# Score matmuls on 64 rows instead of twice 32: q and k transposed as bf16, one head's 64 dims on 64 partitions

## The chip, the cores and the metric

One core of a Trainium2 chip. The metric is device time in microseconds (us), the median of several executions; the profile is one execution, and its span is about 2 us shorter than the time of the same execution. Clock means the share of full speed that TensorE's throttle granted. Engines: PE is TensorE, PEld its loading of weights, DVE VectorE, ACT ScalarE, POOL GpSimd, SP SyncE; a q behind a name (SPq) means the engine's instruction sequencer.

Fast and slow are states of a run: one that is over 1.5% above the fastest run of the same kernel counts as slow and is left out of ratios.

## The reference

```python
# 8 batches, 8 heads, 576 tokens, 64 dims, float32
q_d, k_d, v_d = (x.reshape(B, H, 144, 4, D).mean(axis=3) for x in (q, k, v))   # pooled over 4 tokens
out_d     = softmax(scale * q_d @ k_d.T) @ v_d            # 144 x 144, then repeated 4 times
out_local = softmax(where(|i - j| < 4, scale * q @ k.T, -1e9)) @ v
x = (repeat(out_d, 4) + out_local)                        # -> [4608 tokens, 512]
h = x @ w_in                                              # 512 -> 2048
out = (h * sigmoid(1.702 * h)) @ w_out                    # 2048 -> 512
```

## The kernel before

Tokens are worked on in nine groups of 512. Group g runs the two large products for its tokens (the prediction calls them MoE products) and, between their matmuls, the attention of batch g+1. "The group of batch 2" is group 1, and so on; groups 7 and 8 have no attention. VectorE transposes q and k, GpSimd pools them and v, TensorE computes scores, ScalarE takes exponentials.

A head of q is 576 x 64 numbers: 32 rows of 1152, 18 tokens each. A load by GpSimd brings 4 heads as bf16 onto 128 partitions. In this kernel VectorE transposes 32x32 blocks (one operation of 128x576 fp32 takes 1.24 to 1.25 us); taken as fp32, one element is a pair of bf16 dims. So a head lands on 32 partitions with dims 2p and 2p+1 side by side (the last index, `a`), and each score needs two matmuls of 32 rows that accumulate.

```python
def load_1(name, src, store, b, qd):                # 128 rows, 4 loads a batch (k, q; qd = 0, 1)
    t = ldp.tile([128, 1152], BF16, name=f"{name}b{qd}", tag=f"{name}b{qd}", bufs=2)
    nc.gpsimd.dma_start(out=t, in_=bass.AP(tensor=src.tensor,
        offset=src[b, 4 * qd].offset, ap=[[1152, 128], [1, 1152]]))
    store[b, qd] = t

def prep_1(name, b, qd):                            # 4 fp32 transpositions a batch
    ...
    nc.vector.transpose(out=t32.rearrange("p (i c) -> p c i", c=18),
        in_=store[b, qd].bitcast(FP32).rearrange("p (c d) -> p c d", c=18))

def scores(b, qd, barred=False):                    # 80 matmuls; scores_d (pooled) has 24
    for i in range(5):
        for a in range(2):
            for par in range(2):
                for r in range(4):                  # 4 heads
                    rows = slice(32 * r, 32 * r + 32)
                    nc.tensor.matmul(sp[r // 2][64 * par : 64 * par + 64, r % 2, 60 * i : 60 * i + 60],
                        lhsT=kT[b, qd][rows, k0 : k0 + 64, a], rhs=qT[b, qd][rows, q0 : q0 + 60, a],
                        start=(a == 0 ...), stop=(a == 1 ...), tile_position=(32 * r, 64 * par))
# the order of GpSimd's, VectorE's and SyncE's work in the group of batch b:
    if b > 2: load_v4(b)                            # v in rows of 4 tokens, for pooling (SyncE)
    prep_qk(b, 0); pool_qk(b, 0)
    load_qk(b + 1, 0); load_qk(b + 1, 1)
    prep_v(b); load_v(b + 1)
    prep_qk(b, 1); pool_qk(b, 1)
    prep_v4(b)                                      # pooled v: six operations of GpSimd
```

The softmax here doesn't subtract the row's maximum and nothing guards it: scores larger than these inputs give would overflow.

## Time and profile before

The kernel takes 330.7 us (median of 3 runs, 329.6 to 332.09); the profiled span is 329.5 us at a mean clock of 0.995.

| Quantity | Value | View |
|---|---|---|
| PE busy | 308.0 us, 93% | busy table of the page |
| share of PE in the chain that ended last | 87% | chain of the page |
| groups 1 to 6, start to start | 35.1, 33.7, 33.5, 33.4, 34.3, 33.4 us | starts of each group's first large matmul in the trace |
| a transposition (fp32, 128x576) | 1.24 to 1.25 us | groups of instructions |
| DMA share in a steady group | 0.68 | windows |

The lines of the page, before. First the busy table (time, share of the span, instructions), then the span in 40 slices, a digit being the busy share in tenths, then the chain that ended last:

```profile
PE 308.0 (93%) x4987; PEld 157.9 (48%) x5043; DVE 130.2 (40%) x215; ACT 184.1 (56%) x322; POOL 138.9 (42%) x168
...
PE   8767999789999999999999999998999999999995
...
DVE  4870512770468036802771277225730560000000
...
POOL 7890844049603970298029901990098000000000
PEclk9997999999999999999999999999999999999999
DMA  7999979999814991398339922993180110011011
...
PE 87%; issue 4%; SPq 3%; ACT 2%; DVE 2%; DMA 1%; DVEq 0%; ACTq 0%
```

From the tenth slice on PE is nearly full. VectorE, GpSimd and DMA each have pauses in every group. The costliest groups of instructions that the change touches, before (source line, engine, operation, out<-in, shapes, count | busy us, mean ns | idle before them and its cause):

```profile
L260 DVE STREAM_TRANSPOSE kT<-kb 128x576 f32<-128x576 f32 x16 | 20.0, 1249 | 2.0 <-DMA kb<-in_k_dram 2.0
L260 DVE STREAM_TRANSPOSE qT<-qb 128x576 f32<-128x576 f32 x16 | 19.8, 1239 | 0.9 <-DMA qb<-in_q_dram 0.7
```

The timeline of PE around one block of scores, before (start, length, and the count of matmuls merged into one line), and the windows view of one steady group (stretch, length, busy time of PE, PEld, DVE, ACT and POOL with instructions, clock, DMA share, GB/s; the DMA share adds up the time of packets over 16 engines, and can exceed 1):

```profile
146.25 1.03 PE L618 MATMUL pm<-xT,w_in_bf 128*128 128x512 bf16 x4
147.21 0.84 PE L351 MATMUL pa<-qT,kT 32*64 32x60 bf16 x80
147.85 0.59 PE L370 MATMUL pa<-qdT,kdT 32*64 32x144 bf16 x24
148.38 0.82 PE L618 MATMUL pm<-xT,w_in_bf 128*128 128x512 bf16 x2
```

```profile
135.90:169.40 33.50, 32.60 (x594) 16.88 (x600) 16.30 (x25) 20.95 (x36) 17.53 (x19) 1.00 0.68 144
```

The block of scores occupies PE from 147.21 to 148.38 us. VectorE is busy 16.3 of 33.5 us, GpSimd 17.5.

### The profile page before, as it was taken

To read this page: it belongs to the slowest core of one execution; us is meant where nothing else is said; L and a number is where in the kernel's file an instruction comes from. 1 tells how busy PE (TensorE), PEld (TensorE's weight loads), DVE (VectorE), ACT (ScalarE), POOL (GpSimd) and SP (SyncE) were. 2 spreads that over 40 slices of the span, in tenths; PEclk is the share of its full clock that TensorE was granted. 3 is DMA by queue.
4 is the path that set the end of the run, shared out by engine and by line. 5 is a ranking of instruction groups with operands and counts; after the bars stand their busy time and mean duration, and the time that the engine had idled before them with its cause. 6 is when DMAs were issued, how large, how long until landed. Compare 5 with 4: busy or idle time off the path is not lost.

```text
span 329.5 us, 11220 instructions
## 1 busy us (share of the span) xinstructions
PE 308.0 (93%) x4987; PEld 157.9 (48%) x5043; DVE 130.2 (40%) x215; ACT 184.1 (56%) x322; POOL 138.9 (42%) x168
## 2 busy tenths in 40 slices
PE   8767999789999999999999999998999999999995
PEld 3444455445554455455544555455444544444444
DVE  4870512770468036802771277225730560000000
ACT  2552773375936683667367746674566646415611
POOL 7890844049603970298029901990098000000000
PEclk9997999999999999999999999999999999999999
DMA  7999979999814991398339922993180110011011
GB/s 126 184 188 208 171 151 183 196 210 236 191 39 132 205 207 39 116 193 171 102 100 200 200 83 86 196 195 105 40 172 2 60 41 32 2 72 56 2 62 65
DMA packets 63552, 41.36 MB, mean 126 GB/s; under 512 B 44048, under 2 KB 54416, under 8 KB 63504
## 3 DMA queue, kind: packets, MB, share of 16 engines
q1 hardware_dynamic: 55056, 26.95, 35.8%
q0 software_dynamic: 8304, 13.63, 23.9%
q8 instruction: 39, 0.64, 0.9%
q14 instruction: 9, 0.07, 0.1%
q10 hardware_dynamic: 144, 0.07, 0.1%
HBM read 44.83 MB, written 9.44 MB: 165 GB/s over the span
## 4 chain that ended last, share of the span: by engine, by line
PE 87%; issue 4%; SPq 3%; ACT 2%; DVE 2%; DMA 1%; DVEq 0%; ACTq 0%
PE pm L618 35%; PE pm L674 33%; PE pa L351 3%; SPq L214 3%; PE pa L618 2%; PE pa L431 2%; PE pa L409 2%; PE pa L370 2%; PE pa L458 2%; PE pa L674 2%; DMA vf<-in_v_dram 1%; PE pm L689 1%; PE pa L484 1%; ACT vd L321 0%; PE pa L312 0%
## 5 line engine op out<-in xcount | busy, mean ns | idle before, releaser
L618 PE MATMUL pm<-xT,w_in_bf 128*128 128x512 bf16 x528 | 120.3, 380 | 1.4 <-DVE xT L561 0.7
L674 PE MATMUL pm<-w_out_bf,gT 128*128 128x512 bf16 x493 | 114.1, 379 | 5.4 <-issue 5.2
L629 ACT ACTIVATE gT<-pm 128x512 bf16<-128x512 f32 x136 | 81.0, 598 | 45.2 <-PE pm L618 45.2
L618 PEld LDWEIGHTS <-w_in_bf 128*128 128x128 bf16 x576 | 55.8, 98 | 68.4 <-issue 2.5
L674 PEld LDWEIGHTS <-gT 128*128 128x128 bf16 x560 | 51.7, 98 | 59.5 <-issue 0.2
L276 POOL TENSOR_TENSOR pq<-kT 128x576 f32<-128x576 bf16 x16 | 18.5, 1157 | 105.0 <-DVE kT L260 96.1
L395 DVE TENSOR_TENSOR es<-es,mask 128x600 bf16<-128x600 bf16 x28 | 20.6, 749 | 92.0 <-ACT es L381 91.2
L659 ACT ACTIVATE osb<-pm 128x512 f32<-128x512 f32 (+2 forms) x35 | 20.7, 592 | 40.2 <-PE pm L674 36.1
L534 ACT COPY od<-pa 128x384 f32<-128x384 f32 (+1 forms) x56 | 18.4, 412 | 32.4 <-DVE y L444 18.7
L444 DVE TENSOR_TENSOR y<-pa,rc 128x896 bf16<-128x896 f32 x32 | 34.9, 1092 | 1.1
L555 DVE TENSOR_TENSOR xT<-pa,od 128x570 bf16<-128x570 f32 x28 | 21.1, 753 | 12.0 <-ACT od L534 11.9
L381 ACT ACTIVATE es<-pa 128x600 bf16<-128x600 f32 x32 | 19.8, 668 | 7.0 <-PE pa L351 6.8
L297 POOL TENSOR_TENSOR v<-v 112x512 f32<-112x512 f32 x18 | 22.8, 1265 | 0.0
L661 DVE TENSOR_SCALAR osb<-pm 128x128 f32<-128x128 f32 x1 | 0.3, 292 | 55.3 <-ACT osb L659 55.3
L260 DVE STREAM_TRANSPOSE kT<-kb 128x576 f32<-128x576 f32 x16 | 20.0, 1249 | 2.0 <-DMA kb<-in_k_dram 2.0
L260 DVE STREAM_TRANSPOSE qT<-qb 128x576 f32<-128x576 f32 x16 | 19.8, 1239 | 0.9 <-DMA qb<-in_q_dram 0.7
L276 POOL TENSOR_TENSOR pq<-qT 128x576 f32<-128x576 bf16 x16 | 18.4, 1148 | 0.0
L291 POOL CAST vb<-vf 128x2560 bf16<-128x2560 f32 (+1 forms) x11 | 17.6, 1618 | 0.0
L442 DVE RECIPROCAL rc<-pa 128x14 f32<-128x14 f32 x32 | 7.7, 240 | 21.7 <-PE pa L431 21.7
L351 PE MATMUL pa<-qT,kT 32*64 32x60 bf16 x1280 | 14.0, 203 | 1.5 <-issue 1.5
L351 PEld LDWEIGHTS <-kT 32*64 32x64 bf16 x1280 | 11.8, 104 | 6.7 <-issue 5.5
L300 POOL TENSOR_TENSOR vd<-v 112x256 bf16<-112x256 f32 x18 | 13.7, 759 | 1.4
(90 smaller groups left out, 247.0 us busy)
## 6 DMA issues: line engine op xcount, KB each, us to landing
vf<-in_v_dram SPq DMA_DIRECT2D x80, 128.0 KB, 4.7
out_dram<-osb SPq DMA_DIRECT2D x35, 256.0 KB, 2.1
v<-in_v_dram SPq DMA_DIRECT2D x36, 192.0 KB, 6.1
kb<-in_k_dram POOLq DMA_DIRECT2D x16, 288.0 KB, 6.8
qb<-in_q_dram POOLq DMA_DIRECT2D x16, 288.0 KB, 7.1
w_out_bf<-in_moe_w_out_dram POOLq DMA_DIRECT2D x4, 512.0 KB, 12.1
w_in_bf<-in_moe_w_in_dram POOLq DMA_DIRECT2D x2, 512.0 KB, 5.7
w_in_bf<-in_moe_w_in_dram POOLq DMA_DIRECT2D x1, 1024.0 KB, 10.7
```

The costliest lines, as they stand in the source:

```text
L260: nc.vector.transpose(out=t32.rearrange("p (i c) -> p c i", c=18), in_=store[b, qd].bitcast(FP32).rearrange("p (c d) -> p c d", c=18),)
L276: nc.gpsimd.tensor_tensor(out=t1, in0=sv[:, :, 0:2, :], in1=sv[:, :, 2:4, :], op=ALU.add)
L297: eng.tensor_tensor(out=t1[0:112], in0=x[:, :, 0:2, :], in1=x[:, :, 2:4, :], op=ALU.add)
L351: nc.tensor.matmul(sp[r // 2][64 * par : 64 * par + 64, r % 2, 60 * i : 60 * i + 60], lhsT=kT[b, qd][rows, k0 : k0 + 64, a], rhs=qT[b, qd] ...
L381: nc.scalar.activation(out=es[2 * qd + u][:, :, 0:300], in_=sp[u][:, :, 0:300], func=AF.Exp, scale=inv_sqrt_d,)
L395: nc.vector.tensor_tensor(out=ev, in0=ev, in1=mask, op=ALU.mult)
L444: nc.vector.tensor_tensor(out=y, in0=ov[:, :, :, 0:D], in1=rc.to_broadcast([128, 2, 7, D]), op=ALU.mult,)
L555: eng.tensor_tensor(out=sub(xT[hp], t0 + 3, (57, 2), (114, 5), (1, 57)), in0=sub(x, 3, (509, 2), (57, 5), (1, 57)), in1=sub(od, 3, (57, 2) ...
L618: nc.tensor.matmul(acc, lhsT=w_in_bf[:, dmc, ffc * 128 : (ffc + 1) * 128], rhs=xT[dmc][:, g * TG : g * TG + TG], start=(dmc == 0), stop=(d ...
L629: nc.scalar.activation(out=gT[:, ffc, :], in_=acc, func=AF.Silu, scale=GELU_SCALE)
L659: eng.activation(out=osb, in_=ap, func=AF.Copy, scale=1.0 / GELU_SCALE)
L674: nc.tensor.matmul(ops[t], lhsT=gT[:, ffc, t * 128 : (t + 1) * 128], rhs=w_out_bf[:, ffc, :], start=(ffc == 0), stop=(ffc == n_ffc - 1),)
```

## The change

Its intent: with one head's 64 dims on 64 partitions a score is one matmul of 64 rows, so half of the score matmuls go. To get there, from batch 2 on each row is loaded twice into a pair of 32-partition blocks, the second copy half a token's dims (32 elements) further on, and VectorE transposes bf16 elements, 32 dims of each token. That makes 16 loads a batch (64 rows each) instead of 4, and 8 transpositions instead of 4. v is loaded head by head, and pooled a batch ahead.

```diff
+    ROWS64 = 2
+    def load_2(name, src, store, b, qd):
+        store[b, qd] = []
+        for u in range(2):
+            t = ldp.tile([128, 1152], BF16, ..., bufs=2)
+            store[b, qd].append(t)
+            for j in range(2):
+                nc.gpsimd.dma_start(
+                    out=t[64 * j : 64 * j + 64, 0:1120],
+                    in_=bass.AP(tensor=src.tensor, offset=src[b, 4 * qd + 2 * u + j].offset,
+                        ap=[[32, 2], [1152, 32], [1, 1120]]))
     def prep_1(name, b, qd):
+        if b >= ROWS64:
+            tt = tt.rearrange("p t a -> p (t a)").rearrange("p (u t) -> p u t", u=2)
+            for u in range(2):
+                nc.vector.transpose(
+                    out=tt[:, u].rearrange("p (i c) -> p c i", c=18),
+                    in_=store[b, qd][u].rearrange("p (c d) -> p c d", c=18)[:, :, 0:32])
     def scores(b, qd, barred=False):
+        if b >= ROWS64:
+            for u in range(2):
+                for i in range(5):
+                    for par in range(2):
+                        for j in range(2):
+                            rows = slice(64 * j, 64 * j + 64)
+                            nc.tensor.matmul(sp[u][64 * par : 64 * par + 64, j, 60 * i : 60 * i + 60],
+                                lhsT=kT[b, qd][rows, u, k0 : k0 + 64],
+                                rhs=qT[b, qd][rows, u, q0 : q0 + 60],
+                                start=True, stop=True, tile_position=(64 * j, 64 * par))
     ... scores_d, pool_qk and the uses of pooled v alike ...
@@ the order of the work
             loads_2()
+            prep_v4(2, nc.gpsimd)
         elif b < B:
-            if b > 2:
-                load_v4(b)
+            if b + 1 < B:
+                load_v4(b + 1)
             prep_qk(b, 0)
             pool_qk(b, 0)
             if b + 1 < B:
-                for qd in range(NQ):
-                    load_qk(b + 1, qd)
+                load_qk(b + 1, 0)
+            prep_qk(b, 1)
+            pool_qk(b, 1)
             prep_v(b, nc.gpsimd)
             if b + 1 < B:
                 load_v(b + 1)
-            prep_qk(b, 1)
-            pool_qk(b, 1)
-            prep_v4(b, nc.gpsimd)
+                load_qk(b + 1, 1)
+                prep_v4(b + 1, nc.gpsimd)
```

More of the change, by code (lines that the diff above doesn't have):

```diff
@@ L66 @@
     kdT = [persist.tile([128, 160, 2], BF16, name=f"kdT{i}") for i in range(NQ)]
+    kdP = [persist.tile([128, 2, 160], BF16, name=f"kdP{i}") for i in range(NQ)]
     PA = [psum.tile([128, 2, 512], FP32, name=f"pa{i}") for i in range(3)]
@@ L124, in fill @@
             nc.vector.memset(t[:, SD:160, :], 0.0)
+        for t in kdP:
+            nc.vector.memset(t[:, :, SD:160], 0.0)
         for t in vbs:
@@ L201, in load_1 @@
         store[b, qd] = t
+    def load_2(name, src, store, b, qd):
+        store[b, qd] = []
+        for u in range(2):
+            t = ldp.tile(
+                [128, 1152], BF16, name=f"{name}b{qd}", tag=f"{name}b{qd}", bufs=2
+            )
+            store[b, qd].append(t)
+            for j in range(2):
+                nc.gpsimd.dma_start(
+                    out=t[64 * j : 64 * j + 64, 0:1120],
+                    in_=bass.AP(
+                        tensor=src.tensor, offset=src[b, 4 * qd + 2 * u + j].offset,
+                        ap=[[32, 2], [1152, 32], [1, 1120]],
+                    ),
+                )
     def load_qk(b, qd):
-        load_1("k", k, kf, b, qd)
-        load_1("q", q, qf, b, qd)
+        load = load_1 if b < ROWS64 else load_2
+        load("k", k, kf, b, qd)
+        load("q", q, qf, b, qd)
     def load_v(b, gate=None):
@@ L223, in load_v4 @@
     def load_v4(b):
-        for kc in range(3):
-            for j in range(2):
-                nc.sync.dma_start(
-                    out=v4[64 * j : 64 * j + 48, kc],
-                    in_=bass.AP(
-                        tensor=v.tensor,
-                        offset=v[b, j].offset + kc * 48 * 4 * D,
-                        ap=[[4 * D, 48], [2 * S * D, HP], [1, 4 * D]],
-                    ),
-                )
+        for h in range(H):
+            p0 = 64 * half(b, h // 2, h % 2)
+            nc.sync.dma_start(
+                out=v4[p0 : p0 + 48, :, h // 2, :],
+                in_=bass.AP(
+                    tensor=v.tensor, offset=v[b, h].offset,
+                    ap=[[4 * D, 48], [48 * 4 * D, 3], [1, 4 * D]],
+                ),
+            )
     def load_w_in(c, n):
@@ L254, with half @@
     qT, kT, qdT = {}, {}, {}
+    def half(b, hp, j):
+        return 1 - j if b >= ROWS64 and hp % 2 else j
     def prep_1(name, b, qd):
@@ L258, in prep_1 @@
         tt = work.tile([128, S, 2], BF16, name=f"{name}T{qd}", tag=f"{name}T{qd}", bufs=1)
+        if b >= ROWS64:
[3 more added lines that the diff above has]
+                    out=tt[:, u].rearrange("p (i c) -> p c i", c=18),
+                    in_=store[b, qd][u].rearrange("p (c d) -> p c d", c=18)[:, :, 0:32],
+                )
+            dst[b, qd] = tt
+            return
         t32 = tt.rearrange("p t a -> p (t a)").bitcast(FP32)
@@ L272, in pool_qk @@
             if name not in names:
+                continue
+            if b >= ROWS64:
+                sv = src[b, qd].rearrange("p u (j f) -> p (u j) f", f=4)
+                t1 = work.tile([128, 2 * SD, 2], FP32, name="pq", tag="pq")
+                nc.gpsimd.tensor_tensor(
+                    out=t1, in0=sv[:, :, 0:2], in1=sv[:, :, 2:4], op=ALU.add
+                )
+                if name == "k":
+                    dst = kdP[qd][:, :, 0:SD]
+                else:
+                    dst = work.tile([128, 2, SD], BF16, name=f"qdT{qd}", tag=f"qdT{qd}", bufs=1)
+                    qdT[b, qd] = dst
+                t1 = t1.rearrange("p (u j) f -> p u j f", u=2)
+                nc.gpsimd.tensor_tensor(
+                    out=dst, in0=t1[:, :, :, 0], in1=t1[:, :, :, 1], op=ALU.add
+                )
                 continue
@@ L341, in scores @@
         sp = [ps_tile(), ps_tile()]
+        if b >= ROWS64:
+            for u in range(2):
[3 more added lines that the diff above has]
+                            rows = slice(64 * j, 64 * j + 64)
+                            k0 = 114 * i + KSTART[par]
+                            q0 = 114 * i + QSTART[par]
+                            nc.tensor.matmul(
+                                sp[u][64 * par : 64 * par + 64, j, 60 * i : 60 * i + 60],
+                                lhsT=kT[b, qd][rows, u, k0 : k0 + 64],
+                                rhs=qT[b, qd][rows, u, q0 : q0 + 60],
+                                start=True, stop=True,
+                                tile_position=(64 * j, 64 * par),
+                            )
+            return sp
         if barred:
@@ L363, in scores_d @@
         sd = sd or ps_tile()
+        if b >= ROWS64:
+            for kc in range(3):
+                for u in range(2):
+                    for j in range(2):
+                        rows = slice(64 * j, 64 * j + 64)
+                        pos = half(b, 2 * qd + u, j)
+                        nc.tensor.matmul(
+                            sd[64 * pos : 64 * pos + 64, u, SD * kc : SD * kc + SD],
+                            lhsT=kdP[qd][rows, u, 48 * kc : 48 * kc + 64],
+                            rhs=qdT[b, qd][rows, u, :],
+                            start=True, stop=True,
+                            tile_position=(64 * j, 64 * pos),
+                        )
+            return sd
         bank = sd if sd is PM else [sd[:, u, :] for u in range(2)]
@@ L425, in av_down @@
                     pos = j if x == 0 else 1 - j
+                    r0 = 64 * half(b, hp, j)
                     c0 = 65 * (5 + c2)
@@ L431, in av_down @@
                     nc.tensor.matmul(
-                        o[64 * pos : 64 * pos + 64, j, c0 : c0 + 65],
-                        lhsT=Ed[64 * j : 64 * j + 48, u, q0 : q0 + 64],
-                        rhs=vd[64 * j : 64 * j + 48, kc, hp, :],
+                        o[64 * pos : 64 * pos + 64, r0 // 64, c0 : c0 + 65],
+                        lhsT=Ed[r0 : r0 + 48, u, q0 : q0 + 64],
+                        rhs=vd[r0 : r0 + 48, kc, hp, :],
                         start=(kc == 0), stop=(kc == 2 or last),
-                        tile_position=(64 * j, 64 * pos),
+                        tile_position=(r0, 64 * pos),
                     )
@@ L448, in normalise, with transp @@
         return y
-    def transp(y, n=None):
+    def transp(b, hp, y, n=None):
         x = ps_tile(n)
@@ L469, in transp @@
                     x[64 * j : 64 * j + 64, xx, 288 + 48 * c2 : 336 + 48 * c2],
-                    lhsT=y[64 * pos : 64 * pos + 48, j, 5 + c2, :],
+                    lhsT=y[64 * pos : 64 * pos + 48, half(b, hp, j), 5 + c2, :],
                     rhs=ident[64 * pos : 64 * pos + 48, 0:48],
@@ L608, in f @@
                 for n, hp in enumerate(hps):
-                    st["x", hp] = transp(st["y", hp], slots and slots[n])
+                    st["x", hp] = transp(b, hp, st["y", hp], slots and slots[n])
                 for hp in hps:
```

## The prediction

> **What bounds the kernel.** TensorE. The busy table gives PE 93% of 329.5 us and the chain that ended last is 87% PE. From batch 2 on (one batch per group of about 33.5 us) the timeline of PE shows it waiting for nothing longer than 0.16 us. So PE time removed there counts in full.
>
> **PE time removed.** Each batch has two blocks of 80 score matmuls (32 rows x 64 columns, 60 wide) and 24 pooled-score matmuls (144 wide). In the timeline the block inside the first MoE product runs 147.21 to 148.38 us (1.17 us), the one inside the second product 154.74 to 156.33 us (1.59 us). Most score matmuls start 8.3 ns apart, each with its weight load: a rate of instructions, so halving them should halve that part. The transposes back, 52 matmuls on 64 rows, take 0.78 us until the next MoE matmul (130.79 to 131.57). A new block also has 52 (40 + 12), the 12 wider: I estimate 0.65 to 0.75 us in the first place and 0.9 to 1.0 us in the second. Saved: about 1.1 us a batch, 6 to 6.5 us in six batches. [...] four 64-row matmuls start every 31 ns.
>
> **What is added.** Reads of q/k double: 1024 rows of 4.5 KB a batch instead of 512. A row took about 172 ns of one DMA engine (54 to 60 us), so +5.2 us of all 16 engines a batch. GpSimd issues 16 loads instead of 4, about 0.5 us each: +6 us a batch. VectorE: 8 bf16 transposes instead of 4 fp32 ones (1.25 us each), about the same sum. From batch 3 on this fits: GpSimd would end about 26 us into a group of 32 us, DMA goes from 68% to about 85%.
>
> **What becomes late.** GpSimd runs in order, and the pooling of v for batch 2 (six operations, 6.05 us) now stands in group 0, before the pooling of q/k of batch 2. It waits for the last of eight loads of v4. Before, those loads landed at 75.3 us: DMA is full from 46 to 75 us, first q/k (to 61 us), then v, then v4. The doubled q/k pushes v4 to about 80.5 us. Then 6.05 us of v pooling and 3.7 us of q/k pooling: ready at about 90.2 us. PE wants the pooled scores of batch 2 at about 79.8 us. So it stalls some 10.4 us, once. Its clock then falls: after the idle 2.9 us before 26.4 us, the granted clock was 0.50 at 28 to 30 us[...]. I add 2 us.
>
> **Sum.** 330.7 - 6.3 + 10.4 + 2.2 = 337.0 us; 8 in 10 within 327 to 343. Faster by over 2%: 0.10; within 2%: 0.45; slower by over 2%: 0.45.
>
> **What would show it.** Right: PE idle about 10 us near 80 us before the pooled scores of batch 2, released by GpSimd; GpSimd waiting there for the loads of v4; a dip of the granted clock; score blocks of 0.7 and 0.95 us; groups from batch 3 on about 1.1 us shorter, GpSimd and DMA with room. Wrong: no such stall (then about 324 us), or blocks still over 1.1 us.
>
> **What would make it wrong.** v4 landing several us earlier or later than 80.5; loads of 64 rows[...], so that q/k of later batches are late too; bf16 transposes much slower than fp32; the second block waiting for ScalarE's exponentials.

Three passages are cut out of it. No term of the sum goes with them: 330.7 - 6.3 + 10.4 + 2.2 = 337.0 us stands as recorded. The 2.2 us for the clock are the estimate from one dip in the trace before (0.50 at 28 to 30 us).

## The result, and the profile after

The changed kernel takes 377.1 us (median of 4 runs, 374.54 to 379.75) against 330.15 us for the kernel before in the same rounds: a ratio of 1.142, with a 95% interval of 1.130 to 1.155. Ratios in this document are the mean time of one kernel's fast runs over that of the other's of the same rounds, so they are not quite the ratio of the medians quoted. The prediction was 337.0 us with a range of 327 to 343: far outside.

The same lines of the page, after:

```profile
PE 320.0 (86%) x4419; PEld 155.7 (42%) x4419; DVE 224.5 (60%) x241; ACT 184.4 (49%) x322; POOL 193.1 (52%) x240
...
PE   8749999870497997999699979996999799999996
...
DVE  4853225896075996799569997996579935000000
...
POOL 8861684305999168936892689368913430000000
PEclk9887999995599899999899999998899989999999
DMA  7999499994999988899899988999891001002002
...
DMA 25%; PE 23%; DVE 23%; POOL 18%; SPq 5%; issue 5%; ACT 1%; POOLq 0%; DVEq 0%
```

PE has gone from 87% of the chain to 23%. VectorE, GpSimd and DMA have lost most of their pauses. PE shows one hole, in slices 10 and 11, with a clock of 0.5 in it, and then a dent in almost every group.

```profile
L285 DVE STREAM_TRANSPOSE qT<-qb 128x576 bf16<-128x576 bf16 x24 | 63.9, 2847 | 0.0
L285 DVE STREAM_TRANSPOSE kT<-kb 128x576 bf16<-128x576 bf16 x24 | 62.7, 2795 | 0.0
```

These 48 are of batches 2 to 7 alone (the 8 of batches 0 and 1 stay fp32 and are not among these lines). They take 126.6 us of VectorE, where all 32 took 39.8 before. The block of scores, after, and two neighbouring groups:

```profile
135.15 1.03 PE L697 MATMUL pm<-xT,w_in_bf 128*128 128x512 bf16 x4
136.11 0.51 PE L398 MATMUL pa<-qT,kT 64*64 64x60 bf16 x40
136.45 0.36 PE L434 MATMUL pa<-qdT,kdP 64*64 64x144 bf16 x12
136.74 2.12 PE L697 MATMUL pm<-xT,w_in_bf 128*128 128x512 bf16 x9
```

```profile
160.00:199.00 39.00, 34.50 (x497) 16.33 (x496) 31.16 (x29) 21.06 (x36) 26.78 (x31) 0.96 0.99 162
199.00:235.10 36.10, 32.91 (x498) 16.06 (x497) 33.26 (x28) 21.05 (x36) 26.24 (x31) 1.00 0.94 155
```

The block is 0.63 us long (136.11 to 136.74) instead of 1.17: the saving is there. But the groups are 39.0 and 36.1 us. The waits of PE (engine, line, what it waited for: us in total, times, longest):

```profile
PE pa L434 <- POOL qdT L318: 31.2, 11, 16.4
PE pa L398 <- DVE qT L285: 3.9, 5, 0.9
```

GpSimd's pooling of q, before and after (the last figures are its idle time just before):

```profile
L276 POOL TENSOR_TENSOR pq<-qT 128x576 f32<-128x576 bf16 x16 | 18.4, 1148 | 0.0
L309 POOL TENSOR_TENSOR pq<-qT 128x576 f32<-128x576 bf16 x12 | 16.7, 1395 | 22.1 <-DVE qT L285 22.1
```

In the kernel before GpSimd never waited for a transposed q; now it does, and PE behind it before the pooled q. PE's longest wait is the stall before the pooled scores of batch 2. The timelines of PE and of GpSimd there:

```profile
98.02 0.57 PE L434 MATMUL pa<-qdT,kdP 64*64 64x144 bf16 x12 [16.35 <-POOL qdT L318]
```

```profile
88.17 1.26 POOL L345 TENSOR_TENSOR v<-v 112x512 f32<-112x512 f32 x1 [17.43 <-DMA out_dram<-osb]
...
94.24 1.14 POOL L309 TENSOR_TENSOR pq<-kT 128x576 f32<-128x576 bf16 x1
```

GpSimd waits 17.43 us with the pooling of v, and only then pools q and k. The view puts the wait down to a store that ended last; in the trace's list of DMA issues the last load of v4 landed at about 87.8 us, just before. Groups 1 to 6 are 56.0, 35.2, 39.0, 36.1, 40.7 and 38.4 us long, in sum 42.0 us more than before.

Part of that is the clock. In groups 1 to 6 the trace has 2977 matmuls, as many as that of e_keptsingle below, a kernel with the same matmuls and a clock of 1.00 throughout; PE is busy 206.3 us with them here and 196.1 us there. So about 10 us are matmuls that ran at a lower clock, in groups 1, 3, 5 and 6 (clocks of 0.82, 0.96, 0.92 and 0.96), and the rest is PE standing still.

### The profile page after: what moved, and what is told of

Read it like the earlier page. It is cut to its first block, busy times and chain, and to the rows that moved or that the text cites. A ratio compares the mean times of both kernels' runs of the same rounds, so it can differ in the third digit from the quotient of the medians.

```text
span 373.0 us, 10176 instructions
## 1 busy us (share of the span) xinstructions
PE 320.0 (86%) x4419; PEld 155.7 (42%) x4419; DVE 224.5 (60%) x241; ACT 184.4 (49%) x322; POOL 193.1 (52%) x240
## 4 chain that ended last, share of the span: by engine, by line
DMA 25%; PE 23%; DVE 23%; POOL 18%; SPq 5%; issue 5%; ACT 1%; POOLq 0%; DVEq 0%
DMA qb<-in_q_dram 18%; DVE qT L285 14%; PE pm L753 10%; DVE kT L285 8%; PE pm L697 8%; SPq L235 5%; DMA vf<-in_v_dram 5%; POOL vb L339 4%; POOL pq L309 4%; POOL kb L215 3%; POOL qb L215 3%; DMA v<-in_v_dram 1%; POOL v L345 1%; PE pm L768 1%; PE pm L653 1%
## 5 line engine op out<-in xcount | busy, mean ns | idle before, releaser
L753 PE MATMUL pm<-w_out_bf,gT 128*128 128x512 bf16 x528 | 127.9, 393 | 0.2 <-issue 0.2
L697 PE MATMUL pm<-xT,w_in_bf 128*128 128x512 bf16 x544 | 123.3, 383 | 0.7 <-DVE xT L640 0.7
L285 DVE STREAM_TRANSPOSE qT<-qb 128x576 bf16<-128x576 bf16 x24 | 63.9, 2847 | 0.0
L285 DVE STREAM_TRANSPOSE kT<-kb 128x576 bf16<-128x576 bf16 x24 | 62.7, 2795 | 0.0
L473 DVE TENSOR_TENSOR es<-es,mask 128x600 bf16<-128x600 bf16 x28 | 23.8, 893 | 26.3 <-ACT es L459 25.8
L309 POOL TENSOR_TENSOR pq<-kT 128x576 f32<-128x576 bf16 x12 | 14.4, 1202 | 39.0 <-DVE kT L285 39.0
L215 POOL DMA_DIRECT2D kb<-in_k_dram x48 | 31.7, 679 | 5.2 <-DMA kb<-in_k_dram 4.9
L215 POOL DMA_DIRECT2D qb<-in_q_dram x48 | 31.9, 731 | 2.1 <-DMA qb<-in_q_dram 2.1
L434 PE MATMUL pa<-qdT,kdP 64*64 64x144 bf16 x144 | 5.3, 259 | 31.2 <-POOL qdT L318 31.2
L309 POOL TENSOR_TENSOR pq<-qT 128x576 f32<-128x576 bf16 x12 | 16.7, 1395 | 22.1 <-DVE qT L285 22.1
L465 ACT ACTIVATE ed<-pa 128x864 bf16<-128x864 f32 x15 | 13.5, 898 | 10.3 <-PE pa L434 10.3
```

Of the source, the lines that this page charges most:

```text
L215: nc.gpsimd.dma_start(out=t[64 * j : 64 * j + 64, 0:1120], in_=bass.AP(tensor=src.tensor, offset=src[b, 4 * qd + 2 * u + j].offset, ap=[[3 ...
L285: nc.vector.transpose(out=tt[:, u].rearrange("p (i c) -> p c i", c=18), in_=store[b, qd][u].rearrange("p (c d) -> p c d", c=18)[:, :, 0:32],)
L309: nc.gpsimd.tensor_tensor(out=t1, in0=sv[:, :, 0:2], in1=sv[:, :, 2:4], op=ALU.add)
L473: nc.vector.tensor_tensor(out=ev, in0=ev, in1=mask, op=ALU.mult)
L697: nc.tensor.matmul(acc, lhsT=w_in_bf[:, dmc, ffc * 128 : (ffc + 1) * 128], rhs=xT[dmc][:, g * TG : g * TG + TG], start=(dmc == 0), stop=(d ...
L753: nc.tensor.matmul(ops[t], lhsT=gT[:, ffc, t * 128 : (t + 1) * 128], rhs=w_out_bf[:, ffc, :], start=(ffc == 0), stop=(ffc == n_ffc - 1),)
```

## The experiments

Three theories stood against each other: the slow transpositions make the loss; the pooling of v ahead makes it (with its stall of 16 us); or the doubled loads do. Eighteen kernels ran. They are told in three parts, one for each suspected cause, and a fourth that puts the change together again. "g1" is the group of batch 2, and so on; a kernel's group lengths are of its profiled execution.

### 1. The transpositions

Undo the transposition alone (e_fp32). The rows are loaded so that the second copy starts one element, not 32, further on; the fp32 pair then has dim 2p or 2p+1 in the same place of both copies, and the matmuls use that half of each pair. Matmuls, number of loads and order are the change's. (In this and all later kernels with fp32 pairs, and in e_loads2 and e_loads128, some output tiles have fewer buffers, to make room; e_keptsingle, where PE works 32.65 of 32.70 us, shows no cost of that.)

```diff
-   out=t[64 * j : 64 * j + 64, 0:1120], ... offset=src[b, 4 * qd + 2 * u + j].offset,
-       ap=[[32, 2], [1152, 32], [1, 1120]]
+   out=t[64 * j : 64 * j + 64], ... offset=src[b, 4 * qd + 2 * u + j].offset - 1,
+       ap=[[1, 2], [1152, 32], [1, 1152]]
-   transpose(out=tt[:, u] (18 apart), in_=store[b, qd][u] (bf16, 32 of each 64))
+   transpose(out=t32 of tt (18 apart), in_=store[b, qd][u].bitcast(FP32))
+   dst[b, qd] = tt[..., 1]        # the same half of every pair
```

> The changed kernel with one thing undone: the second half of the rows is loaded one element apart instead of 32, so that VectorE can transpose pairs of bf16 as fp32 (as the kernel before does) and every second token element holds the 64 dims. Loads, row count, order and score matmuls stay. Theory 1 (the slow bf16 transposes, 2.5 us each, 20 us a batch, make q/k of groups 2 to 6 late): a transpose takes about 1.1 us, the stalls before the scores of groups 2 to 6 vanish, these groups fall from 189 us together to about 163 us; the stall of 16 us in group 1 stays; total about 350 us. Rival (the doubled loads bind: q/k land late, or GpSimd's 16 load issues): groups 2 to 6 stay above 35 us each and the total above 365 us.

Measured: 351.6 us (350.85 to 352.87), ratio 1.066 [1.059, 1.072], which is 25.5 us less than the change (377.1). A transposition is back at 1.24 us, though there are still 8 a batch:

```profile
L285 DVE STREAM_TRANSPOSE kT<-kb 128x576 f32<-128x576 f32 x24 | 28.1, 1244 | 2.5 <-DMA kb<-in_k_dram 2.5
```

The stall of g1 stayed (15.77 us), the waits for qT and for the pooled q of the second half are gone, and g5 and g6 ran in 32.6 and 32.5 us. Groups 2 to 6 took 169.3 us together: far from the 189 of the change, but not the 163 expected.

e_fp32 also shifts the loads by some elements, so the reverse was run too: slow transpositions alone, put in front of the fp32 ones of the kernel before from batch 2 on (e_slowtr).

```diff
+        if b >= 2:
+            for n in (18, 9):      # bf16, 18 and 9 blocks, into a scratch tile
+                nc.vector.transpose(out=scr[:, 0 : 32 * n] (n apart),
+                    in_=store[b, qd] (bf16, 32 of each 64)[:, 0:n])
```

> The kernel before plus dummy bf16 transposes into a scratch tile, one of 18 blocks and one of 9 in front of each fp32 transpose from batch 2 on, so that VectorE spends about as long on them as in the changed kernel; loads, order and scores as before. Theory 1: VectorE's transposes alone cost about 3 to 5 us a group from batch 2 on: 345 to 360 us. Rival (transposes are hidden unless the loads are doubled too): within 2% of before.

Measured: 360.92 us (359.09 to 363.21), ratio 1.094 [1.086, 1.102]: some 30 us, a little over the 345 to 360 expected, without any other part of the change. Its groups 2 to 6 ran in 38.2 to 39.5 us, at clocks of 0.91 to 0.96; in each PE waited about 3 us for the pooled v of GpSimd, which had waited for VectorE.

What exactly is slow? e_micro adds 18 transpositions into the kernel before, two of each kind, in a group without attention, where VectorE has nothing else to do.

```diff
+   for src, dst in ((fp32 pairs, spread), (bf16 gapped, spread), (bf16 dense, spread),
+                    (bf16 gapped, dense), (bf16 dense, dense), (fp32 pairs, dense),
+                    (bf16 36 blocks, dense), (bf16 9 blocks, spread), (bf16 gapped, 4-byte slots)):
+       for _ in range(2): nc.vector.transpose(out=dst, in_=src)
```

> The kernel before with 18 extra transposes on VectorE in the second last group, where VectorE is idle, two each of: fp32 18 blocks spread output (about 1.1 us start to start), bf16 as in the change (2.5), bf16 dense input spread output, bf16 gapped input dense output, bf16 dense both, fp32 dense both, bf16 36 blocks dense both, bf16 9 blocks as in the change, bf16 with output elements 4 bytes apart in pairs. Theory a (2-byte elements written apart are the slow part): dense output brings bf16 to 0.7 us. Theory b (2-byte transposes are slow in any layout): all bf16 ones stay at about 2.5 us. Time of the kernel unchanged.

The timeline of VectorE in e_micro, one of each pair; the lines are fp32 spread; bf16 gapped in, spread out; bf16 dense in, spread out; bf16 gapped in, dense out; fp32 dense; bf16 with 36 blocks, dense; and bf16 written spread into 4-byte slots:

```profile
272.65 1.25 DVE L859 STREAM_TRANSPOSE sc<-kb 128x576 f32<-128x576 f32 x1
...
275.22 2.65 DVE L859 STREAM_TRANSPOSE sc<-kb 128x576 bf16<-128x576 bf16 x1
...
280.58 2.65 DVE L859 STREAM_TRANSPOSE sc<-kb 128x576 bf16<-128x576 bf16 x1
...
285.95 0.78 DVE L859 STREAM_TRANSPOSE sc<-kb 128x576 bf16<-128x576 bf16 x1
...
289.20 0.78 DVE L859 STREAM_TRANSPOSE sc<-kb 128x576 f32<-128x576 f32 x1
...
290.83 1.38 DVE L859 STREAM_TRANSPOSE sc<-kb 128x1152 bf16<-128x1152 bf16 x1
...
296.63 2.70 DVE L859 STREAM_TRANSPOSE sc<-kb 128x576 bf16<-128x576 bf16 x1
```

Gaps in the input cost nothing (2.65 with and without). What costs is 2-byte elements written apart: 2.65 us against 0.78 us for the same elements written side by side. 4-byte elements written apart (every 72 bytes) cost 1.25 against 0.78. Giving each 2-byte element a 4-byte slot of its own, so that they too stand every 72 bytes instead of 36, does not help (2.70), so in these forms it is the size of the element, not where it stands. (A single run of 333.31 us, of unknown state; the comparison is within one execution.)

Between the dense bf16 outputs, 576 elements more cost 1.38 - 0.78 = 0.60 us, 1.04 ns each. The spread 2-byte outputs are far from that: 2.65 us for 576 elements are 4.6 ns each on average, so an estimate of 0.6 us per 576 elements, taken from the dense ones, would be short by 2 us.

### 2. The order: v pooled ahead

e_order2 undoes the order for batch 2 alone: its v is pooled in g1 after its q and k.

```diff
             loads_2()
-            prep_v4(2, nc.gpsimd)
 ...
-            if b + 1 < B:
+            if b > 2 and b + 1 < B:
                 load_v4(b + 1)
 ...
             prep_v(b, nc.gpsimd)
+            if b == 2:
+                prep_v4(2, nc.gpsimd)
+                load_v4(3)
```

> The changed kernel with v of batch 2 pooled in group 1, after q/k of batch 2, instead of in group 0. Theory 2 (the 16.35 us stall before the pooled scores of batch 2 comes from GpSimd's order: it waits for v4 first): that stall falls below 1 us, and some 5 to 8 us come back later in group 1, at the products with v, since v4 lands only near 88 us and the transposes are slow: total 366 to 370 us. Rival (q/k of batch 2 themselves are late, by the doubled loads or slow transposes): the stall at that place stays over 8 us.

Measured: 372.67 us (369.84 to 380.66), ratio 1.124 [1.115, 1.134]; a gain of about 4.5 us, less than the 16 us of the stall that it was to remove and less than the 7 to 11 expected. Its profiled execution was slow and is not compared. So where the rest of the stall's time went is not shown; that the slow transpositions take it back in other waits is a guess.

e_orderalone does the reverse, on the kernel before: v4 loaded and pooled a batch ahead, nothing else.

```diff
             loads_2()
+            prep_v4(2, nc.gpsimd)
 ...
-            if b > 2:
-                load_v4(b)
+            if b + 1 < B:
+                load_v4(b + 1)
 ...
-            prep_v4(b, nc.gpsimd)
+            if b + 1 < B:
+                prep_v4(b + 1, nc.gpsimd)
```

> The kernel before with only the order changed: v4 loaded and pooled a batch ahead, so v of batch 2 is pooled in group 0 before q/k of batch 2. Loads and transposes as before. Theory 2: v4 lands at about 75 us, v is pooled by 81.5, q/k of batch 2 by 85.2: one stall of about 5 us before the pooled scores of batch 2, no others; total about 336 us. Rival (the order is harmless without doubled loads): no stall, within 2 us of before.

Measured: 336.53 us (334.95 to 337.95), ratio 1.020 [1.011, 1.030]: the total as expected, but not the way to it. The stall before the pooled scores of batch 2 is 2.56 us where 5 were expected, there are others, and g1, with a clock of 0.96, is 40.1 us instead of 35.1. So the order by itself costs about 6 us even with single loads.

### 3. The matmuls saved, and the doubled loads

First the saving by itself (e_half): the second of each pair of accumulating matmuls is left out in the kernel before from batch 2 on. The scores are wrong. They passed the check's tolerance, as did those of every kernel here that is wrong, so a passed check alone does not prove a layout right.

```diff
-            for a in range(2):
+            na = 1 if b >= 2 else 2
+            for a in range(na):
```

> The kernel before with the second of each pair of accumulating score matmuls left out from batch 2 on (32 rows of 64; wrong numbers on purpose): the 624 matmuls gone, nothing else changed. Theory (the score matmuls are paced by the number of instructions and all of that time is on the chain): about 1.1 us less a group, 6 to 7 us in all, 323 to 325 us. Rival (other waits take it back): within 2 us of before.

Measured: 323.81 us (321.23 to 325.27), ratio 0.981 [0.973, 0.990]; groups 2 to 6 all take 32.5 us. The sum that the prediction gave for the matmuls, 6 to 6.5 us, is borne out: the medians differ by 6.8 (330.6 before), and the interval of the ratio spans 3.5 to 9 us.

Next the change with both mends (e_best): fp32 pairs, and batch 2's v pooled in its own group. Batch 2 itself keeps the old layout here; batches 3 to 7 have the new one.

```diff
-    ROWS64 = 2
+    ROWS64 = 3
     ... as e_fp32; batch 2: prep_v4(2), load_v4(3), load_qk(3, 0) after its q/k are pooled ...
```

> The changed kernel with fp32 transposes (as in e_fp32), from batch 3 on instead of 2, and v of batch 2 pooled in group 1 after its q/k. No 16 us stall, no stalls from transposes; five groups with halved scores. If only the named causes were at work: 330 - 5.5 = 324.5 us. If the fetches of instructions under the full DMA cost as much as in e_fp32 (some 2.5 us in each of three groups): about 331 us, no gain.

(Late fetches of instructions, here and in later expectations, are theory; what the traces show of them is told with e_single.)

Measured: 344.24 us (343.67 to 350.14), ratio 1.043 [1.035, 1.052]: neither. With both mends some 20 us remain over the 323.8 of the saving alone. PE's stalls are now at instructions that wait for no semaphore.

Are those the doubled loads? Adding loads to the kernel before was tried three times.

```diff
 e_loads:    from batch 2 on, each load_1 followed by two more 64-row loads into 2 scratch tiles
 e_loads2:   the same into 4 scratch tiles
 e_loads128: each load_1 followed by one more load of 128 rows (same bytes, 8 loads a batch)
```

> The kernel before with eight extra loads of 64 rows a batch from batch 2 on, into a scratch tile (1024 rows a batch in all, as in the change); order, transposes and scores as before. Theory 3 (the doubled loads cost by themselves little: v4 of batch 2 lands at 82 to 88 us instead of 75, which delays its pooled v by a few us once, and instruction fetches of TensorE come late now and then): 333 to 340 us. Rival (they bind): each group over 35 us, total over 345 us.

> The kernel before with eight extra loads of 64 rows (two halves, as in the change) a batch from batch 2 on, into four scratch tiles, so that no load waits for another one's tile (the run e_loads had only two and blocked GpSimd by that). Theory 3 (what is left in e_best, 344 us where 324.5 was hoped for, comes from the doubled loads, which delay TensorE's fetches of instructions): stalls of TensorE of 1 to 3 us at instructions that wait for no semaphore, 338 to 345 us. Rival (the loads cost nothing as long as q/k arrive in time): within 1% of before.

> As e_loads2, but the extra rows are loaded as four loads of 128 rows a batch, in the form of the kernel before. Same number of rows, nearly the same bytes. Theory 3a (the form counts: a load of 64 rows in two halves makes 464 extra packets of 4 bytes[...]): less than half the cost of e_loads2, 332 to 336 us. Theory 3b (the bytes count): as e_loads2.

(A clause is cut from it: on how many DMA engines a load's packets ran, no run shows.)

e_loads took 475.36 us (ratio 1.442) and was a flawed experiment: loads into the same scratch tile wait for each other, and GpSimd stood still behind them, 21 to 25 us a group. e_loads2 took 381.19 us (1.149) for a related reason: a load's issue waits until the load eight before it has landed (the trace shows eight semaphores in turn, and 40.6 us of GpSimd's waits for landed loads), and 12 loads a batch are more than eight, so GpSimd stood before the pooling of q and k. e_loads128 is the clean one: 341.77 us (341.08 to 345.33), ratio 1.031 [1.023, 1.039]. The doubled bytes alone cost about 10 us, with never more than eight loads a batch.

e_best32 splits each 64-row load of e_best into two of 32 rows, since 37,424 packets of 4 bytes had come with the 64-row loads.

```diff
-            for j in range(2):     # out=t[64 * j : 64 * j + 64], two copies in one load
+            for j in range(4):     # out=t[32 * j : 32 * j + 32], one copy in each
```

> e_best with each load of 64 rows cut into two of 32 rows, one half each: same bytes, 32 loads a batch for GpSimd to issue. Theory 3a: packets of 4 bytes fall from some 37,000 to under 5,000, the stalls at instructions without a semaphore wait mostly vanish: 328 to 335 us, if the issues (an estimated 0.5 us each, 16 us a group) do not make GpSimd late. Theory 3b: stays at 344 us.

Measured: 349.74 us (346.31 to 351.08), ratio 1.051 [1.043, 1.060]. The packets of 4 bytes fell to 2,864 and a load of half the size landed after 4.5 to 5.4 us (median) instead of 11.5 to 12.6. But 32 issues of 0.49 us made GpSimd late (PE waited 5.75 and 5.53 us for the pooled q in two groups), and the total did not gain. The run changes both at once, so it does not tell what the small packets cost; that e_loads128 pays about as much for doubled bytes without them (10 us; e_best over e_single below: 9) speaks against them as the main cause. Why a load of half the size lands in less than half the time, no run here shows; the trace does not name the DMA engines of a load.

Could the layout pay where DMA is idle? e_late uses it for batches 6 and 7 only, with everything before as in the kernel before.

```diff
-    ROWS64 = 2
+    ROWS64 = 6
     ... order of the kernel before up to batch 4, of e_best from batch 5 on ...
```

> The kernel before up to batch 5; only batches 6 and 7 have their q/k as one head on 64 partitions, with the fp32-pair transposition and the rows loaded one element apart, and v pooled a batch ahead from batch 6 on (the order changes in the group of batch 5). In the version that did this from batch 3 on, the last group (batch 7) ran 32.5 us instead of 33.4, and in the one with only the transposition mended the last two groups ran 32.6 and 32.5 us. Theory (the matmuls saved are real, what the doubled loads cost is that they come while the DMA engines and the instruction fetches are busy, group after group): the last two groups run about 32.6 us each instead of 34.3 and 33.4, the group of batch 5 loses 0 to 1.5 us to the doubled loads of batch 6, and the whole takes 327 to 330.5 us, no more than the kernel before. Rival (each batch with doubled loads costs some 2 to 4 us whatever else goes on): 332 to 336 us.

Measured: 336.15 us (334.54 to 342.32), ratio 1.011 [1.006, 1.017]. The last group ran in 32.5 us as hoped, but the groups of batches 5 and 6 in 36.1 and 36.9 instead of 33.4 and 34.3: in the latter PE waited 2.66 us for the pooled q. The total is that of the rival (its upper end). It does not prove the rival's reason, because in these two groups the order changes as well: in that of batch 5 GpSimd pools the v of two batches.

Then the direct test: take the doubled loads away and leave all the rest. In e_single (from e_best) and e_aftersingle (from the change itself), q and k are loaded once, 4 loads of 128 rows; both transpositions read the same tile, so the numbers are wrong, with the same instructions on all engines but GpSimd's issues. e_split is e_single with each load issued as four of 32 rows.

```diff
-        for u in range(2): t = ldp.tile(...); store[b, qd].append(t)
-            for j in range(2): nc.gpsimd.dma_start(out=t[64 * j : 64 * j + 64], ...)
+        t = ldp.tile(...); store[b, qd] = [t, t]
+        nc.gpsimd.dma_start(out=t, ...)                         # e_single, e_aftersingle
+        for j in range(4): nc.gpsimd.dma_start(out=t[32 * j : 32 * j + 32], ...)   # e_split
```

> e_best (fp32-pair transposition, v of batch 2 pooled after its q/k, halved matmuls) with q/k of every batch loaded once, 4 loads of 128 rows as in the kernel before; both transpositions read the same tile, so the numbers are wrong on purpose, with the same instructions on TensorE, VectorE and in the pooling. Theory (the doubled loads are the whole residual of e_best): 324 to 327 us, groups from batch 3 on 32.5 us, stalls at instructions without a semaphore wait gone. Rival (something else of the change costs it, such as 8 transpositions a batch or the pooled outputs): 338 to 344 us, the stalls as in e_best.

> e_single, but each of the 4 loads a batch issued as four loads of 32 rows: 16 issues a batch as in the change, bytes not doubled; wrong numbers on purpose. If the bytes of the doubled loads make the residual: within 2 us of e_single. If the 16 issues by GpSimd and their waits for one of eight slots make it: within 3 us of e_best (341 to 347), with GpSimd late before the pooled scores.

> The changed kernel with q/k loaded once (4 loads of 128 rows a batch), all else as it is: slow bf16 transpositions, v of batch 2 pooled first; wrong numbers on purpose. If the three causes add up: 377 less about 20, 355 to 359 us; the stall in the group of batch 2 shrinks from 16.4 to about 5 to 10 us (v4 lands near 75 us again), the waits for qT and the pooled q of the second half (0.9 and 2.6 us a group) stay, since they come from the transpositions. If doubled loads count only together with other delays: 365 us or more.

e_single: 334.96 us (333.76 to 336.15), ratio 1.010 [1.004, 1.016]. e_split: 332.42 us (331.45 to 333.77), ratio 1.003 [0.998, 1.009]. So the doubled bytes cost about 9 us here (344.2 less 335.0), and the 16 issues cost nothing by themselves (e_split is even 2.5 us faster than e_single). But 335 is neither number that was expected: both theory and rival failed. The groups of batches 3 to 7 took 32.5 to 34.2 us; what was left lay in g1, 42.5 us. The timeline of PE in e_single there, and the windows view over the same time, e_single and then the kernel before:

```profile
93.65 0.24 PE L511 MATMUL pa<-vd,ed 48*64 48x65 bf16 x5 [2.39 <-issue]
...
101.22 0.29 PE L511 MATMUL pa<-vd,ed 48*64 48x65 bf16 x10 [3.74 <-issue]
```

```profile
90.00:95.00 5.00, 2.45 (x87) 1.47 (x87) 1.15 (x3) 1.70 (x2) 0.00 (x0) 1.00 1.10 232
95.00:100.00 5.00, 2.48 (x79) 1.27 (x76) 2.92 (x5) 0.60 (x1) 0.16 (x1) 1.00 1.21 216
```

```profile
90.00:95.00 5.00, 4.65 (x173) 2.71 (x171) 3.08 (x6) 1.88 (x2) 0.00 (x0) 1.00 0.23 81
95.00:100.00 5.00, 4.68 (x116) 2.45 (x112) 3.71 (x7) 1.81 (x5) 0.00 (x0) 1.00 0.03 7
```

PE stalls 2.39 and 3.74 us in the middle of a run of short matmuls ("issue": nothing in the profile released it) while the DMA engines are full (shares of 1.10 and 1.21) with batch 3's v4, v, q and k. In the kernel before they were almost idle at that time. A 16 KB packet of the instruction queue landed during each of the two stalls, 1.4 to 1.5 us before PE went on. This is hardly chance: the 20 traces kept have 74 stalls of PE over 1 us for which the profile shows no semaphore, and every one ends 1.2 to 1.8 us after an instruction packet landed, though a trace has only 34 to 39 of these. So PE very likely waited for instructions. That the other transfers held these up is argued only from where the stalls lie (e_keptsingle has two, both before 28 us, e_best eight, spread up to 245 us); no run isolates it.

e_aftersingle: 372.56 us (369.25 to 375.53), ratio 1.121 [1.112, 1.129]. It was expected at 355 to 359 if causes add up; they do not. The stall of g1 shrank as expected (5.61 us), but every group stayed at 37 to 43 us. The last one with attention shows why. No q or k is loaded in it (DMA share 0.16), and yet it takes 37.1 us, at a clock of 1.00:

```profile
271.50:308.60 37.10, 31.98 (x491) 15.94 (x496) 30.90 (x29) 21.06 (x36) 10.44 (x9) 1.00 0.16 57
```

VectorE starts the transpositions when it has done its last merge of the group before, and works on them for 20 us (272.01 to 291.65 in the timeline); then PE waits 0.9 us for qT and 2.55 us for the pooled q. Here the slow transpositions set the group's length, with hardly a load beside them.

### 4. The change put together again

What remained open was whether the order made the 9 us of g1 in e_single, and what the doubled loads cost in the order of before. e_keptsingle is the changed kernel with fp32 pairs, single loads (wrong numbers) and the order of the kernel before. e_kept has the doubled loads, right results, and v pooled in its own group; the second half of the loads comes after it. e_last issues all 16 loads after it.

```diff
 e_keptsingle: load_v4(b) first, loads after pool_qk(b, 0), prep_v4(b) last, as before; q/k loaded once
 e_kept:   prep_qk/pool_qk(b, 0); load_qk(b + 1, 0); prep_qk/pool_qk(b, 1); prep_v(b);
           load_v(b + 1); prep_v4(b); load_qk(b + 1, 1)
 e_last:   as e_kept, with load_qk(b + 1, 0) moved to the end, before load_qk(b + 1, 1)
```

> The changed kernel with the fp32-pair transposition, q/k loaded once (wrong numbers on purpose), and the loads and the pooling of v in the order of the kernel before; 8 transpositions, halved matmuls and pooled outputs of the change stay. If the order of loads and pooling makes the 9 us left in the group of batch 2: 323 to 326 us, as with the matmuls halved alone (323.8), the group of batch 2 at 33 to 34 us. If something else of the change makes them (8 transpositions, v4 loaded head by head): 331 to 335 us.

> The changed kernel with the fp32-pair transposition and v pooled in its own batch's group as before; only the loads of the next batch's second half of q/k are issued last in the group, after the pooling of v. Right results. If the doubled loads cost about 10 us whatever the order (e_best less e_single: 9 us; 128-row loads of the same bytes added to the kernel before: 10 us): 332 to 337 us, not faster than the kernel before. If they cost only where they meet the new order: 324 to 328 us, a version that beats both.

> e_kept with all 16 loads of the next batch's q/k issued by GpSimd at the end of its work in the group, after the pooling of v; right results. In e_kept the pooled v of a group ended 177.5 us where TensorE needed it by about 174; 5.3 us less makes it timely. Theory (what doubled loads cost here is GpSimd's time ahead of the pooled v, and a smaller part by late instruction fetches while the DMA engines are full): no wait for the pooled v from batch 3 on, groups of 33 to 35 us, 328 to 338 us. Rival (the doubled bytes themselves make everything late, in whatever order): q/k land too late for the next group's transpositions, TensorE waits for the pooled q/k, 345 us or more.

e_keptsingle: 326.53 us (325.36 to 326.77), ratio 0.989 [0.987, 0.991]. A little above the expected 323 to 326 in the median, but far from the rival's 331 to 335: the order made most of the 9 us (about 1 us of it is batch 2, which has the old layout in e_single). One of its steady groups:

```profile
134.10:166.80 32.70, 32.65 (x497) 15.91 (x496) 21.75 (x29) 20.84 (x36) 17.91 (x19) 1.00 0.70 147
```

PE works 32.65 of 32.70 us. Eight fp32 transpositions a batch, the pooling in the new layout and v4 by heads all fit. Groups 1 to 6 are 197.1 us in sum against 203.5 before; between the medians of the whole kernels only 3.5 us are left (the profiled execution of the kernel before, at 331.33 us, was not its quickest, and in e_keptsingle group 1 starts 0.6 us later).

e_kept: 358.18 us (354.7 to 358.87), ratio 1.084 [1.077, 1.090], far above both numbers expected. PE's longest wait in total names a part of the reason:

```profile
PE pa L511 <- POOL vd L349: 14.4, 10, 2.0
```

GpSimd issued eight loads (5.3 us, 159.48 to 164.7 in its timeline) ahead of the pooling of v, and the pooled v came late in groups 1 to 5. These 14.4 us are not all: groups 1 to 6 are 31.8 us longer than in e_keptsingle. PE is busy about 11 us longer with the same matmuls, at clocks of 0.91 to 0.96 in groups 1 to 5, and the rest is other waits. e_last takes those out of the way, and the theory behind it falls too: 390.35 us (387.3 to 393.01), ratio 1.175 [1.170, 1.180]. The waits of GpSimd and of PE in e_last:

```profile
POOL kb L215 <- DMA kb<-in_k_dram: 41.1, 15, 6.9
```

```profile
PE pa L511 <- POOL vd L349: 27.7, 17, 1.9
```

From the first issue to the last, the 16 loads take 18 us (143.50 to 161.1 in GpSimd's timeline), 5.38 and 1.25 us of it waits for a load eight before; a load lands 12 to 13 us after its issue (median). Issued last, q and k arrive after the next group wants them, GpSimd reaches its pooling late, and so again the pooled v, and the pooled q (10.4 us of PE's waits); the clock is 0.84 to 0.92 in groups 1 to 6.

Taken one after the other, these kernels divide the difference of 47 us (medians; the kernel before had medians of 330.0 to 331.4 us beside them, so each term is good to 1 or 2 us):

| Kernel | Time, us | Step |
|---|---|---|
| before | 330 | |
| e_keptsingle: matmuls halved, 8 fp32 transpositions, old order, single loads | 326.5 | -3.5 |
| e_single: and v4 and loads moved ahead (batch 2 pools v after q/k) | 335.0 | +8.4 |
| e_best: and doubled loads (batch 2 in the old layout in this one and the one above) | 344.2 | +9.3 |
| e_fp32: and batch 2 in the new layout, with doubled loads, its v pooled before its q/k | 351.6 | +7.4 |
| the change: and bf16 transpositions | 377.1 | +25.5 |

The terms hold on this path only: e_aftersingle shows that with slow transpositions the doubled loads cost 4.5 us between medians, not 9, and e_kept that in an order near the old one they cost over 30 (no run has the old order itself with doubled loads). Each step holds the lower clock that came with it.

## Why the prediction was wrong

- "Saved: about 1.1 us a batch, 6 to 6.5 us in six batches." Right. The blocks shrank as costed (0.63 us where 0.65 to 0.75 was estimated, from 1.17), e_half gave 6.8 us between medians, and the six groups of e_keptsingle are 6.4 us shorter than before. The rate of starts that the prediction read from the trace before (four matmuls of 64 rows every 31 ns) held for the new matmuls: in the trace after, four of 64 rows start every 32 ns, while each is put at about 0.2 us.
- "VectorE: 8 bf16 transposes instead of 4 fp32 ones (1.25 us each), about the same sum." This is the step that failed most. It counted a bf16 transposition as half of an fp32 one, without saying why; yet each has as many elements as an fp32 one. A bf16 transposition written 18 elements apart takes 2.65 us (e_micro; 2.80 and 2.85 on average in the changed kernel), so VectorE had 21 us a batch instead of 5. GpSimd waited 22.1 us for transposed q (0.0 before), and PE for the pooled q behind it. Undone, it gives back 25.5 us (e_fp32); alone it costs some 30 (e_slowtr). The prediction had named it among what would make it wrong, but gave it no time in its range. A duration should have been marked as unknown, since no bf16 transposition stood in the trace before.
- "PE ... stalls some 10.4 us, once", behind the pooling of v. The mechanism was right: the stall, its place, its releaser and GpSimd's wait are in the trace after, with a clock of 0.50 from 83.8 to 100.9 us in the windows view, as after the idle 2.9 us in the trace before (0.50 at 28 to 30 us). The size was off: 16.35 us, since v4 landed at 87.8 us and not at 80.5. The term mis-sized is the transfer time of the doubled q and k: the prediction added the rows' time on 16 engines, 5.2 us, and v4 came 12.5 us later than before (75.3). GpSimd issued batch 2's 16 loads from 53.1 to 70.1 us, and the last landed at 84.7 us; before, they were there by about 61.
- "From batch 3 on this fits: GpSimd would end about 26 us into a group of 32 us, DMA goes from 68% to about 85%." This failed. The DMA share was 0.99 and 0.94 in the groups shown, and even with fast transpositions and a better order the doubled loads cost 9 us (e_best less e_single), or 10 as plain bytes added to before (e_loads128). The sum for GpSimd was about right (busy 26.8 and 26.2 us in the two groups shown). But a sum of busy times was held against the length of a group; what counts is when each load lands and what GpSimd does after it. In e_kept and e_last the same 16 loads, moved within the group, cost 32 and 64 us over e_keptsingle.
- "I add 2 us" for the clock: right in kind, too small. The matmuls of groups 1 to 6 took about 10 us longer than the same ones at a clock of 1.00 in e_keptsingle; about 3 of these lie in g1, around the stall that was foreseen, the rest in groups 3, 5 and 6, where the prediction had no stalls.
- The range of 327 to 343 us reckoned with one stall and a full PE around it. It left no room for a VectorE that sets the length of every group, nor for what the causes do together.

Two things stay open: whether it is the full DMA engines that make instruction packets late, and so stall PE in e_single and e_best; and which stall is followed by a lower clock. In groups 3 and 6 after, 3.2 and 3.3 us of waits for the pooled q came with clocks of 0.96, in the last group of e_aftersingle 3.3 us of the same waits with 1.00.

No version with right results beat the kernel before. The layout with fast transpositions is worth 3.5 us (e_keptsingle, 1.1%), if its loads cost nothing, and with its doubled loads the kernel was slower than before in every order tried, if only by 1.1% in e_late, where two batches have them.

## What to carry to other kernels

Before counting on an operation in another element size or access pattern, measure that very form once by itself: the same 576 elements took 0.78, 1.25 or 2.65 us, depending only on how the output was written and how wide its elements were. An engine with room on average can still be what everything waits for (GpSimd, busy 52% of the changed kernel's span, kept PE waiting 31.2 us for the pooled q), so ask of each added load or operation which instruction stands behind it in the same in-order queue, and when. And if several mends are tried, take away each cost alone from the changed kernel too: here, where VectorE set the length of the groups, the costs did not add (e_aftersingle took 372.56 us, where a sum of causes gave 355 to 359).
